# A two-layer mixer on one core: block-diagonal first stage for the filter, small vectors as rows, the MLP's first tokens in the written order

## The chip, the core and the metric

The kernel runs on one core of a Trainium2 chip. A core has five engines with an instruction stream each: PE (TensorE, matrix products into PSUM), DVE (VectorE), ACT (ScalarE), POOL (GpSimd) and SP (SyncE, which here issues nearly all DMAs). PE writes only to PSUM, and only DVE and ACT copy results out of it ("evacuate" it) into SBUF. The engines wait for one another through semaphores. The metric is the device time of one execution in microseconds; before the change the median of three runs is 253.25 us (252.85 to 253.61).

## The reference

Input and output are 2048 tokens of 512 values in bf16. Two kinds of layers alternate, A, B, A, B, each with a residual sum around it:

```python
def _A_ref(q, k, v, shift_k, ssm_k, ssm_D):
    k_shift = sum over t < 4 of k[s - t] * shift_k[:, t]     # four taps per channel
    kv = k_shift * v
    y = irfft(rfft(kv, 4096) * rfft(ssm_k, 4096))[:2048]     # long causal convolution, per channel
    return q * (y + kv * ssm_D)

def _B_ref(x, w1, b1, w2, b2):
    return gelu(layernorm(x) @ w1 + b1) @ w2 + b2            # 512 -> 1376 -> 512

x = A_q
x = x + _A_ref(_layernorm(x), A_k, A_v, ...)
x = x + _B_ref(_layernorm(x), B_w1, ...)
x = x + _A_ref(_layernorm(x), A_k, A_v, ...)
x = x + _B_ref(_layernorm(x), B_w1, ...)
```

(The listing is cut and its sums are put in short.) Everything in A but its q is the same for both A layers, so y is computed once.

## The kernel before

The work has two parts. The first computes y, in an order that is written out by hand; the second runs both MLPs over four groups of 512 tokens each, twice (eight rounds).

**First part.** The long convolution is a transform of 2048 = 32 x 64 points done with products. For kv and for the filter A_ssm_k alike, a first stage multiplies by a small table (32 points), a second by twiddled tables (64 points); the two spectra are multiplied, and two more stages go back. The 512 channels go in four chunks of 128, numbered cc = 0 to 3. The pieces have names, and a piece that ends in "e" is the evacuation of the piece without the "e":

- lk, lv, lK, lx, lM, lW, lX, w1, w2 and so on: loads, issued by SP. lSK loads a row of A_shift_k, lsT the same data as columns, lb0 and lb1 the MLP's bias as columns.
- kT: transposes of k (PE); dg: diagonal matrices from the taps; kv: the four taps as products with these diagonals; kvm: the product with v (DVE). Channels of chunk 3 take another way: POOL's multiplications kg, ka, kgm with the taps spread by bSK.
- U{cc}S: first stage of kv, U{cc}T its transposes (chunk 3 by DMA); KS{c}{g}: first stage of the filter, sixteen pieces; K2: its second stage; sa, sb: two DMA copies that swap halves.
- X{cc}{j}: second stage of kv; T{cc}{j}: the multiplication of the spectra (DVE); V{cc}{j}: the third stage; Z and TA to TD: turns, by DMA or PE; Y: the last stage.
- s00, s01, s02: statistics, scale and application of the first norm of tokens 0 to 511; s10, s11 the statistics and scale for tokens 512 to 1023. g, h, p, b: gating, statistics, scale and application of the second norm of tokens 0 to 511, in units of 1, 1 and 2 tiles of 128 tokens; LT their transposes for the MLP.

The string ORDER sets the order: a word such as `KS11.P3` or `U2T1e.A` names a piece, its engine (S, P, D, A, G for POOL) and, for PE, which of four PSUM buffers of 1024 columns it takes. Each engine runs its pieces in that order; the waits follow from what is read and written. All big arrays lie in one SBUF tile, `arena`, at byte offsets given by hand, and a place is used again by other data as the work goes on. The row of A_ssm_D, which the filter needs early, is parked in it ahead of everything else, with a DMA that ACT issues (L186), and POOL copies it into the tile Dz (L194):

```python
SKr = at(82 * K, [[1, P * KS]], 0, 1)
nc.scalar.dma_start(apf(arena, 40 * K, [[32 * ROW, 4], [1, D]]), apf(A_ssm_D, 0, [[0, 4], [1, D]]))
```

`at` counts bytes and `apf` counts elements of two bytes, so the second line's 40 K is byte offset 80 K; its four rows lie on partitions 0, 32, 64 and 96.

**Second part.** A round multiplies by W1 (L686; eleven tiles of 128 columns, four products each), applies gelu on ACT with the bias (L688), and multiplies by W2 (L720); DVE adds the result to x (L725). Two rounds ahead, `prep` does the norms of a group on DVE, with one small power on POOL, and turns it by DMA (L712). Round 0 is cut in three units that follow the end of the first part.

Of the kernel before, what the change touches and what calls it, by code (L numbers as in the profile page):

```python
# [29 lines left out]
def _make_tables():  # L30
# [43 lines left out]
    F = np.concatenate([F2, np.tile(KF, (4, 1))], axis=1)  # L74
# [30 lines left out]
def kernel(ctx: ExitStack, tc: tile.TileContext, A_q, A_k, A_v, A_shift_k, A_ssm_k, A_ssm_D,  # L105
                 B_x, B_w1, B_b1, B_w2, B_b2, out):
    nc = tc.nc
    P = 128
# [55 lines left out]
    SKr = at(82 * K, [[1, P * KS]], 0, 1)  # L164
    one = const.tile([1, P], BF16, name="one")
    kh = const.tile([P, KS - 1, P], BF16, name="kh")
    sT = const.tile([P, CT, KS], BF16, name="sT")
# [641 lines left out]
```

## Time and profile before

| | |
|---|---|
| median of the runs | 253.25 us |
| span of the profiled execution | 251.9 us |
| its own time | not on the page; taken to be that of the runs, so that some 1.3 us lie around the span |
| first part, until the first product of L720 | 106.4 us |
| seven and a half rounds after it | 145.5 us |
| PE, DVE, ACT, POOL busy, share of the span | 94%, 67%, 58%, 22% |
| granted PE clock | full throughout |

A row of the timeline gives the start, the time, the engine and line, the operation, what is written and read, and in brackets how long the engine had been idle and what ended that. A "q" after an engine (SPq, ACTq) marks the issue of a DMA. A share of busy time is an average over stages that have different limits, so the stages are looked at one by one.

### The profile page before, as it was taken

The numbers are of one execution on the slowest core, as the hardware profiler recorded it, in microseconds if no ns is written. First come the engines' busy times: TensorE is split into PE (matmuls) and PEld (weight loads), VectorE is DVE, ScalarE is ACT, GpSimd is POOL, SyncE is SP. The second block draws the span as 40 slices with busy tenths as digits, with TensorE's granted clock in tenths as the row PEclk, the third lists the DMA queues.
The fourth block names the chain that finished last, engine by engine and source line by source line (L and its number), as shares of the span: only waits on it lengthen the run. The fifth ranks groups of instructions, "written<-read, shape, count | busy, mean of one in ns | idle before, by whom it ended". The sixth has DMA issues, their size and how long they took to land.

```text
span 251.9 us, 5135 instructions
## 1 busy us (share of the span) xinstructions
PE 236.9 (94%) x2104; PEld 146.1 (58%) x2104; DVE 169.7 (67%) x319; ACT 146.5 (58%) x212; POOL 54.6 (22%) x52
## 2 busy tenths in 40 slices
PE   2688999999999999999999999999999999999995
PEld 1588767899998738844444444444444444444443
DVE  0335889989999794987889899886866862022022
ACT  3598899999999798903803803803703712712810
POOL 3199999510000011011111101110110110000000
DMA  5999994698929993022040403107006006001001
GB/s 130 367 349 183 239 428 191 209 390 300 232 44 181 175 318 113 0 48 39 1 83 0 86 0 61 22 0 86 1 28 139 3 25 143 0 23 64 0 21 62
DMA packets 53040, 30.15 MB, mean 120 GB/s; under 512 B 46642, under 2 KB 50456, under 8 KB 51736
## 3 DMA queue, kind: packets, MB, share of 16 engines
q1 hardware_dynamic: 52864, 29.73, 45.0%
q8 instruction: 16, 0.26, 0.4%
q10 hardware_dynamic: 152, 0.09, 0.1%
q14 instruction: 8, 0.07, 0.1%
HBM read 16.71 MB, written 2.10 MB: 75 GB/s over the span
## 4 chain that ended last, share of the span: by engine, by line
PE 70%; DVE 9%; ACT 8%; DMA 8%; issue 4%; ACTq 0%; SPq 0%; DVEq 0%
PE po L720 30%; PE ph L686 29%; DVE arena L218 4%; DMA arena<-in_A_q_dram 3%; DMA arena<-in_B_w_dram 3%; DVE T L555 2%; PE p L506 2%; PE p L336 2%; ACT arena L216 2%; ACT ZT L216 2%; DVE ZT L218 2%; DMA arena<-in_A_ssm_D_dram 2%; ACT xb L216 2%; ACT arena L469 1%; PE p L382 1%
## 5 line engine op out<-in xcount | busy, mean ns | idle before, releaser
L688 ACT ACTIVATE arena<-ph,B 128x512 bf16<-128x512 f32 (+5 forms) x110 | 63.5, 609 | 81.9 <-PE ph L686 81.8
L686 PE MATMUL ph<-arena 128*128 128x512 bf16 (+4 forms) x440 | 78.5, 336 | 0.9 <-DMA arena<-in_B_w_dram 0.5
L720 PE MATMUL po<-arena 128*128 128x512 bf16 (+2 forms) x363 | 77.4, 372 | 0.0
L686 PEld LDWEIGHTS <-arena 128*128 128x128 bf16 (+1 forms) x440 | 40.5, 100 | 38.0 <-DMA arena<-in_B_w_dram 1.0
L720 PEld LDWEIGHTS <-arena 128*128 128x128 bf16 (+1 forms) x363 | 35.4, 98 | 40.5
L725 DVE TENSOR_TENSOR arena<-po,arena 128x512 bf16<-128x512 f32 (+1 forms) x33 | 21.5, 673 | 43.6 <-PE po L720 43.6
L216 ACT ACTIVATE arena<-p 128x1024 bf16<-128x1024 f32 (+6 forms) x40 | 38.8, 1040 | 7.9 <-PE p L423 4.5
L250 POOL TENSOR_TENSOR lrsm<-lrsm,mhalf 128x4 f32<-128x4 f32 (+2 forms) x10 | 8.9, 885 | 96.6 <-DVE lrsm L244 96.6
L216 ACT ACTIVATE ZT<-p 128x1024 bf16<-128x1024 f32 (+1 forms) x22 | 21.6, 1038 | 0.1
L238 DVE BATCH_NORM_STATS2 lstm<-arena 128x6 f32<-128x512 bf16 x32 | 19.9, 681 | 0.2
L218 DVE CAST arena<-p 128x1024 bf16<-128x1024 f32 x15 | 17.8, 1221 | 1.6 <-PE p L382 1.4
L555 DVE TENSOR_TENSOR T<-xb,arena 128x2048 bf16<-128x2048 bf16 (+1 forms) x17 | 18.8, 1163 | 0.0
L564 PE MATMUL p<-arena,T 128*128 128x128 bf16 x256 | 16.5, 219 | 1.1 <-DVE arena L218 0.4
L250 POOL TENSOR_TENSOR lrsg<-lrsg,mhalf 128x4 f32<-128x4 f32 x8 | 8.1, 1014 | 40.8 <-DVE lrsg L247 40.8
L437 POOL TENSOR_TENSOR T<-arena,SK 128x2048 bf16<-128x2048 bf16 (+3 forms) x4 | 15.0, 3751 | 5.1 <-DMA arena<-in_A_k_dram 5.0
L216 ACT ACTIVATE xb<-p 128x1024 bf16<-128x1024 f32 x15 | 15.9, 1132 | 0.1
L564 PEld LDWEIGHTS <-T 128*128 128x128 bf16 x256 | 14.9, 98 | 1.7 <-issue 1.4
L238 DVE BATCH_NORM_STATS2 lstg<-arena 128x6 f32<-128x512 bf16 x24 | 14.8, 680 | 0.0
L218 DVE COPY arena<-p 128x2048 bf16<-128x2048 bf16 (+3 forms) x10 | 10.4, 1049 | 5.9 <-issue 3.7
L255 DVE TENSOR_SCALAR arena<-arena,lmvg,lrsg 128x512 bf16<-128x512 bf16 x28 | 9.7, 408 | 6.7 <-POOL lrsg L250 6.7
L255 DVE TENSOR_SCALAR arena<-arena,lmvm,lrsm 128x512 bf16<-128x512 bf16 x32 | 11.2, 409 | 2.3 <-POOL lrsm L250 2.3
L506 PE MATMUL p<-DG,arena 128*128 128x128 bf16 x192 | 11.4, 219 | 1.3 <-ACT ZT L216 0.9
(78 smaller groups left out, 222.8 us busy)
## 6 DMA issues: line engine op xcount, KB each, us to landing
arena<-arena SPq DMA_DIRECT2D x8, 512.0 KB, 4.5
arena<-in_A_k_dram SPq DMA_DIRECT2D x4, 512.0 KB, 6.7
arena<-in_A_v_dram SPq DMA_DIRECT2D x2, 1024.0 KB, 10.8
arena<-in_A_ssm_k_dram SPq DMA_DIRECT2D x4, 512.0 KB, 7.1
arena<-tabM SPq DMA_DIRECT2D x1, 2048.0 KB, 12.5
arena<-in_A_q_dram SPq DMA_DIRECT2D x1, 2048.0 KB, 9.1
out_dram<-arena SPq DMA_DIRECT2D x15, 128.0 KB, 1.7
arena<-in_B_w_dram SPq DMA_DIRECT2D x1, 1376.0 KB, 7.8
```

Source lines behind the costliest of these rows:

```text
L216: nc.scalar.activation(dst, src, AF.Copy)
L218: nc.vector.tensor_copy(dst, src)
L238: nc.vector.bn_stats(self.st[:, i, 0, :], x_t[:, GT * g + i, :] if src is None else src[:, i, :])
L250: nc.gpsimd.tensor_tensor(self.rs[:, a:b], self.rs[:, a:b], mhalf[:, a:b], ALU.pow)
L255: nc.vector.tensor_scalar(out=dst[:, i, :], in0=xs, scalar1=self.mv[:, i, 0:1], scalar2=self.rs[:, i:i + 1], op0=ALU.subtract, op1=ALU.mult)
L506: nc.tensor.matmul(o[:, i, :], w, DG[:, cc, t, :], start=t == 0, stop=t == KS - 1)
L555: eng.tensor_tensor(view(Tb[it["slot"]["T"]], [2, n, CW]), x2, kk, ALU.mult)
L564: nc.tensor.matmul(o[:, i, :], T[:, r, i, :], Mt[:, ka + i, 1 - r, :], start=r == 0, stop=r == 1)
L686: nc.tensor.matmul(o.rearrange("p (i t) -> p i t", t=P), W1t[:, ct, ft * P:ft * P + m], lt[:, a:b, ct, :], start=ct == 0, stop=ct == CT - 1)
L688: nc.scalar.activation(hT[0:m, ft, a * P:b * P], o, AF.Gelu_apprx_tanh, bias=B1[0:m, ft:ft + 1])
L720: nc.tensor.matmul(po[:, a:b], hT[0:m, ft, i * P:(i + 1) * P], W2t[0:m, ft, a:b], start=ft == 0, stop=ft == FT - 1)
L725: nc.vector.tensor_tensor(xs, po[:, a:b], xs, ALU.add)
```

## The change

- The table for the filter's first stage becomes block-diagonal: one product of all 128 rows with 256 columns takes the place of four pieces of 32 rows and 64 columns; the product with the identity that came ahead of each group (L377) goes. A step handles four blocks for all rows instead of eight for half of them.
- The taps are loaded as one row of 2048 values and turned to columns by twelve products with one column each (bS); the bias likewise by eleven (bB). The loads lsT, lb0, lb1 in columns and POOL's copies sF and B1 go.
- The MLP's first 512 tokens (transposes LT1, LT2, products M, gelu Me) come into the written order and use its PSUM buffers.
- x is loaded in two pieces (lx, ly); the statistics of tokens 512 to 1023 (LG1) are taken from ly at the end of the first part instead of from a load of their own; the separate load lx1 and s10, s11 go.
- The order is another.

SP's first loads before, in order (the word behind "waits" is the semaphore; DMAHW0 to DMAHW7 are eight DMA semaphores that are used in turn, DMAHW1 first by the load of A_ssm_D):

```order
L280 DMA arena<-in_A_shift_k_dram 1x512
L280 DMA arena<-in_A_k_dram 128x2048
L280 DMA sT<-in_A_shift_k_dram 128x4x4
L280 DMA arena<-in_A_k_dram 128x2048 x3
L280 DMA kh<-in_A_k_dram 112x3x128 [waits DMAHW0_49]
```

and in the changed kernel:

```order
L279 DMA arena<-in_A_shift_k_dram 1x2048 [waits DMAHW1_49,Pool_49]
L279 DMA arena<-in_A_k_dram 128x2048 x4
L279 DMA kh<-in_A_k_dram 15x3x128
L279 DMA kh<-in_A_k_dram 112x3x128 [waits DMAHW0_49]
L279 DMA arena<-in_B_b_dram 1x1376
```

The first load has got a wait for the load of A_ssm_D and for POOL, since its row now begins at 80 KB; the load of sT is gone, and the bias comes early.

ACT's work behind the statistics s00, before (ZT is the first stage of kv, 128x64x8x2 are the filter's pieces KS):

```order
L472 ACTIVATE arena,aq_124<-arena,as_123 128x512 x4
L216 ACTIVATE ZT_95<-p_119 128x4x8x32
L216 ACTIVATE ZT_95<-p_121 128x4x8x32
L490 ACTIVATE arena<-arena,am_125,lrsg_106 128x512 x4
L216 ACTIVATE ZT_96<-p_122 128x4x8x32
```

and after:

```order
L423 ACTIVATE DG<-IDt,sF 128x128 x12
L215 ACTIVATE arena<-p_117 128x4x3x128
L475 ACTIVATE arena,as_121<-arena 128x512 x4
L476 ACTIVATE as_121<-as_121 128x4
L478 ACTIVATE arena,aq_122<-arena,as_121 128x512 x4
L215 ACTIVATE ZT_93<-p_117 128x4x8x32
L215 ACTIVATE ZT_94<-p_119 128x4x8x32
L215 ACTIVATE ZT_94<-p_120 128x4x8x32
```

The application of the first norm (L490, s02) has left ACT; it stands on DVE behind the last multiplication T. The diagonals (DG) have come to ACT. In the same way U2T1e has gone from ACT to DVE.

ACT at the end of the first part, before (ph are the PSUM tiles of the MLP) and after (p the four buffers of the first part):

```order
L216 ACTIVATE arena<-p_122 128x1024
L216 ACTIVATE arena<-p_120 128x1024
L216 ACTIVATE arena<-p_121 128x1024
L688 ACTIVATE arena<-ph,B_77 128x128 x8
L216 ACTIVATE arena<-po 128x512
L688 ACTIVATE arena<-ph,B_77 128x128 x2
L688 ACTIVATE arena<-ph,B_77 96x128
```

```order
L215 ACTIVATE arena<-p_118 128x1024
L697 ACTIVATE arena<-p_119,B_76 128x128 x2
L697 ACTIVATE arena<-p_119,B_76 96x128
L697 ACTIVATE arena<-p_117,B_76 128x128 x8
L215 ACTIVATE arena<-p_118 128x1024
L215 ACTIVATE arena<-p_120 128x512
L697 ACTIVATE arena<-p_119,B_76 128x256 x4
```

The first gelu pieces now stand between the evacuations of Y instead of behind all of them, and the tokens come in the order 128 to 255, 256 to 511, 0 to 127.

The diff, cut to its core:

```diff
 ORDER = """
-lSK.S lk1.S lsT.S lk3.S lk0.S lk2.S bSK.P3 lh1.S bSKe.A lh113.S lx0.S kT1.P2 lv0.S sF.G lv1.S dg0.D dg2.D ...
+lSK.S bSK.P0 bSKe.A bS.P2 lk3.S lk1.S lk0.S lk2.S lh113.S bSe.A dg2.A dg0.A dg1.A lh1.S kg0.G kT3.P2 ...
 """
-    F = np.concatenate([F2, np.tile(KF, (4, 1))], axis=1)
+    F = np.concatenate([F2, np.kron(np.eye(4), KF)], axis=1)
...
-    SKr = at(82 * K, [[1, P * KS]], 0, 1)
+    SKr = at(80 * K, [[1, D * KS]], 0, 1)
+    b1r = at(85 * K, [[1, FT * P]], 0, 1)
...
-        lS = [load("lsT", sT[:], A_shift_k.rearrange("(ct p) k -> p ct k", p=P), 2 ** 17),
-              load("lSK", SKr, apf(A_shift_k, CK * P * KS, [[P * KS, 1], [1, P * KS]]), 2 ** 13)]
+        lS = [load("lSK", SKr, apf(A_shift_k, 0, [[D * KS, 1], [1, D * KS]]), 2 ** 13),
+              load("lb1", b1r[:, 0:F], apf(B_b1, 0, [[F, 1], [1, F]]), 2 ** 13)]
...
-        sf = plan.add("sF", {"G": 100}, lS[:1], lambda it: nc.gpsimd.tensor_copy(sF[:], sT[:]))
+
+        def columns(o):
+            for ct in range(CK):
+                for t in range(KS):
+                    nc.tensor.matmul(o[:, ct * KS + t:ct * KS + t + 1], at(80 * K + 2 * (ct * P * KS + t), [[KS, P]], 0, 1),
+                                     one[0:1, 0:1], start=True, stop=True)
+        _, sf = mm_evac("bS", 700, lS[:1], columns, [CK * KS], lambda: sF[:])
...
-                    nc.tensor.matmul(o[:, 0, :, :].rearrange("p m k -> p (m k)")[:, 0:320], IDt[:], Ft[:], start=True, stop=True)
-                    for m in range(8):
-                        for e in range(2):
-                            rs = slice(64 * g + 32 * e, 64 * g + 32 * e + 32)
-                            s0 = 16 * c + 2 * m
-                            nc.tensor.matmul(o[:, e, m, :], Kd[rs, s0:s0 + 2, :].rearrange("p s b -> p (s b)"), Ft[rs, 256:320],
-                                             start=True, stop=True)
...
+                    for m in range(4):
+                        s0 = 2 * (m0 + m)
+                        nc.tensor.matmul(o[:, m, :], Kd[:, s0:s0 + 2, :].rearrange("p s b -> p (s b)"), Ft[:, 256:512],
+                                         start=True, stop=True)
...
-        s10, _ = first(1, x1, lx1)
...
-        lx = load("lx", x_t[:], q_d.rearrange(TOK, p=P), 2 ** 21, USp)
+        lx = load("lx", x_t[:, 0:GT, :], xd[:, 0:GT, :], 2 ** 19, USp)
+        ly = load("ly", x_t[:, GT:, :], xd[:, GT:, :], 3 * 2 ** 19, USp)
...
+        def head(n, part, f0, f9, deps):
...
+            pe = plan.add(f"M{n}{part}", {"P": 218 * (b - a) * (f9 - f0)}, deps, mms, take=["ps"])
...
+                    nc.scalar.activation(hT[0:m, ft, a * P:b * P], o[0:m, ft - f0, :], AF.Gelu_apprx_tanh, bias=B1[0:m, ft:ft + 1])
+            plan.add(f"M{n}{part}e", {"A": 250 * (b - a) * (f9 - f0)}, [pe, sb] + wd, gelu, free=[(pe, "ps")])
...
+        plan.add("LG1", {"D": 2950}, [ly], lambda it: (LG[1].part(1, 0, GT), LG[1].join(0, GT)))
...
-                for (a, b), nxt in zip(UNITS, UNITS[1:] + (None,)):
-                    mm1(0, a, b, 0, FT - 3)
...
+                one_ = prep(1)
+                LG[1].scale(0, GT)
+                for f in one_[1:] + pr[:1]:
+                    f()
                 mm2(0, 0, False, pr[1:])
```

More of the change, by code (lines that the diff above doesn't have):

```diff
@@ L404 @@
                        for w, a in (("a", 0), ("b", 1))])
-        _, bSK = mm_evac("bSK", 250, lS[1:2], lambda o: nc.tensor.matmul(o, one[:], SKr, start=True, stop=True), [P * KS],
+        _, bSK = mm_evac("bSK", 250, lS[:1], lambda o: nc.tensor.matmul(o, one[:], SKr[:, CK * P * KS:], start=True, stop=True), [P * KS],
                          lambda: SK[:])
@@ L455, in stats @@
             return plan.add(name, {"D": 670 * (b - a) + 150 + 40 * (b - a)}, deps, fn)
-        x1 = view(Tb[1], [GT, D])
         xd = q_d.rearrange(TOK, p=P)
         lx0 = load("lx0", lna0, xd[:, 0:GT, :], 2 ** 19)
-        lx1 = load("lx1", x1, xd[:, GT:2 * GT, :], 2 ** 19)
         def first(n, x, ld):
@@ L491, in first @@
             return s0, plan.add("s02", {"D": 1350, "A": 2200}, [s1], apply) if n == 0 else s1
-        _, s2 = first(0, lna0, lx0)
-        s10, _ = first(1, x1, lx1)
+        s0, s2 = first(0, lna0, lx0)
+        for it in sum(KX, []):
+            it["deps"] += [s0, bSK, sf, sb]
         kvp, USp, ZU = [], [], []
@@ L641 @@
         UNITS = (0, 1), (1, 2), (2, 4)
+        norm = []
         for n, (a, b) in enumerate(UNITS):
@@ L661 @@
             gb = plan.add(f"b0{a}", {"D": 350 * m}, [gp], lambda it, a=a, b=b: LM[0].apply(lnx[0], 0, a, b))
+            norm.append(gb)
             if n == 0:
-                mm_evac("LT0", 240, [gb], lambda o: turn_x(o, 0, 1), [1, CT, P], lambda: lnT[0][:, 0:1, :, :], True,
-                        edeps=wd, rank=1)
+                lt0 = mm_evac("LT0", 240, [gb], lambda o: turn_x(o, 0, 1), [1, CT, P], lambda: lnT[0][:, 0:1, :, :], True,
+                              edeps=wd, rank=1)[1]
         for g in range(1, 4):
```

69 lines of the change are left out of this document (41 added, 28 removed).

## The prediction

> **What bounds the kernel now.** I read the view by windows first, then the chain that ended last, then the timeline of the first 20 us, and last ScalarE (ACT) by itself. The windows are cut where the stages meet; after the two times stand the busy us of PE, PE's weight loads, VectorE (DVE), ACT and POOL, then the granted PE clock, the DMA share and GB/s.
>
> ```profile
> core 0 of [0], span 251.9 us
> 0.00:13.22 13.22, 5.63 (x49) 4.39 (x50) 2.42 (x13) 6.21 (x6) 4.21 (x18) 1.00 0.81 257
> 13.22:19.95 6.73, 6.40 (x104) 6.15 (x105) 3.09 (x4) 6.26 (x18) 6.73 (x3) 1.00 1.04 302
> 19.95:30.00 10.05, 9.18 (x176) 7.99 (x176) 7.06 (x6) 8.09 (x11) 9.64 (x9) 1.00 1.14 190
> 30.00:82.37 52.37, 50.20 (x879) 43.98 (x872) 49.26 (x51) 51.82 (x57) 18.61 (x9) 1.00 0.82 252
> 82.37:106.40 24.03, 22.86 (x244) 17.48 (x242) 18.51 (x37) 20.96 (x45) 2.32 (x4) 1.00 0.62 153
> 106.40:251.90 145.50, 142.59 (x671) 66.06 (x669) 89.33 (x213) 53.17 (x79) 13.09 (x13) 1.00 0.19 41
> ```
>
> From 106.4 us to the end PE does nothing but the MLP:
>
> ```profile
> 86.98 7.79 DMA arena<-in_B_w_dram
> ...
> 106.37 9.51 PE po L720 x44
> 115.89 9.50 PE ph L686 x44
> ```
>
> Phases of 9.5 us follow each other without a gap. The change adds or removes no product there, so I cost this part at nothing: the kernel gains or loses exactly by how much the first product of L720 moves from 106.37 us. Ahead of it, between 30 and 82.37 us, ACT is busy 51.82 of 52.37 us, more than PE (50.20, with modelled ends) and DVE (49.26). ACT's list of PSUM evacuations is therefore my measure of that stretch, not PE.
>
> The span is 251.94 us and the median of the runs 253.25, so 1.3 us lie outside the first and last instruction; I leave them as they are and take differences from the median.
>
> **The change part by part: the head.** The rows are those of the first 17 us.
>
> ```profile
> 0.80 0.35 SPq L280 DMA_DIRECT2D arena<-in_A_shift_k_dram  x1
> 1.18 1.21 ACTq L186 DMA_DIRECT2D arena<-in_A_ssm_D_dram  x1
> 1.21 0.38 SPq L280 DMA_DIRECT2D arena<-in_A_k_dram  x1
> 2.11 0.58 PE L407 MATMUL p<-arena,one 1*128 1x512 bf16 x1 [2.11 <-DMA arena<-in_A_shift_k_dram]
> 5.25 0.19 POOL L192 MEMSET arena<- 128x96 bf16 x1 [3.20 <-DMA arena<-in_A_ssm_D_dram]
> 5.37 1.41 POOL L194 COPY Dz<-arena 1x128 bf16<-1x128 bf16 x4
> 8.85 15.70 SPq L353 DMA_DIRECT2D arena<-in_A_ssm_k_dram  x4
> 11.89 0.85 PE L423 MATMUL p<-IDt,arena 128*128 128x128 bf16 x12 [0.28 <-DMA arena<-in_A_k_dram]
> 16.01 1.23 DVE L512 TENSOR_TENSOR arena<-p,arena 128x1024 bf16<-128x1024 f32 x1 [2.21 <-DMA arena<-in_A_v_dram]
> ```
>
> The new row of A_shift_k is 4 KB at 80 KB of partition 0, exactly where the row of A_ssm_D is parked (the old 1 KB row lay at 82 KB). So SP's first load now waits until A_ssm_D has landed and POOL has made its first copy of it; behind it in SP's queue stand all loads of k, q, v and the filter. When does it go? A_ssm_D is issued at 1.18; it lands at 2.5 at the earliest (a small load took 2.11 - 0.80 = 1.31 us) and at 5.2 as now. Now it shares the engines with SP's loads; then it is alone behind one table, which took 1.9 us to land (below). I take 1.18 + 1.9 = 3.1, plus 0.19 and one copy of 1.41 / 4 = 0.35: 3.65 us. The first load of k follows 0.41 later at 4.06 instead of 1.21: 2.85 us late (2.3 to 5.0).
>
> Against that, the small pieces go: the load of sT (512 pieces of 8 bytes) stood between the first two loads of k.
>
> ```profile
> 2.00:4.00 2.00, 0.58 (x1) 0.00 (x0) 0.00 (x0) 1.57 (x3) 0.05 (x1) 1.00 0.92 228
> 4.00:6.00 2.00, 0.47 (x5) 0.47 (x6) 0.00 (x0) 0.40 (x1) 0.71 (x3) 1.00 0.68 139
> 8.00:10.00 2.00, 1.12 (x11) 1.13 (x12) 1.11 (x7) 0.48 (x1) 0.00 (x0) 1.00 1.03 407
> ...
> Ft<-tabF ACTq DMA_DIRECT2D x1, 80.0 KB, 1.9
> sT<-in_A_shift_k_dram SPq DMA_DIRECT2D x1, 4.0 KB, 4.5
> ```
>
> While sT was on its way the engines moved 139 GB/s, later 407. The 2.1 MB of k are now complete 11.89 - 1.21 = 10.7 us after the first issue. Without sT I take 0.55 us to the first byte, 2 us at 300 GB/s, the other 1.5 MB at 407 (3.7 us) and 1.7 us to the signal: 8.0 us, so 12.05 instead of 11.89, and with what follows (a transpose batch of 0.85, eleven one-column products for the MLP's bias ahead of the convolution on PE) I take +0.4 us. The ends: nothing recovered +2.85, or +5.0 with the late landing; all at 407 GB/s, -0.5. *By a rule of the Trainium skill (DMA: Bandwidth & Descriptors, Specifications) transfers under 512 bytes are done as read-modify-write; by it the slow stretch belongs to sT, and the term would be about +0.2; the 139 GB/s row agrees, but does not part it from a slow start of the loads themselves.*
>
> The diagonals move from DVE to ACT and wait for twelve one-column products instead of sT. Prices: a one-column product between 0.02 us (16 pieces in 0.34, below) and 0.1, so bS and bB at most 1.2 us each; a diagonal on ACT between the 2.0 / 12 that it cost on DVE and 2.18 / 8.
>
> ```profile
> L417 DVE TENSOR_SCALAR DG<-IDt,sF 128x128 bf16<-128x128 bf16 x12 | 2.0, 248 | 7.1 <-POOL sF L361 7.1
> 95.31 2.18 ACT L688 ACTIVATE arena<-ph,B 128x128 bf16<-128x128 f32 x8 [0.82 <-PE ph L686]
> ```
>
> A_shift_k arrives at 3.65 + 1.31 = 4.96, bSK and bS end by 6.7, twelve diagonals at 0.27 by 10.0: before the last k, which hides them. The second load of v now stands behind two filter loads of 15.70 / 4 = 3.9 us of SP each, so it is issued near 16.5 and lands about 22; the new order asks for it only at 23 (all first halves of the convolution come first). If that cover fails it costs 1 to 2 us of DVE.
>
> **Filter's first stage.** PE's pieces of the chain:
>
> ```profile
> 24.73 0.87 PE p L304 x8
> ...
> 35.53 0.24 PE p L377
> 35.77 0.34 PE p L382 x16
> ```
>
> A step was 0.34 + 0.24 = 0.58 us; it becomes four products of the shape of L304, 0.87 / 2 = 0.44. Sixteen steps give PE back 2.2 us, less about 0.7 for the bias. The evacuation stays 1024 columns per step, on ACT or DVE, so PE waits for it: on the path this is worth nothing by itself. *The Trainium skill (TensorE: Matmul & The Clock Gate, Part 3) says the opposite of this change: four products of 32 rows each run side by side, 3.07 times as fast. Worked out as an estimate, the full-array form would cost 0.34 x 3.07 = 1.04 us per step, 7.4 us more over sixteen, and the kernel would be slower. The rows of L304 decide against it: that shape takes 0.44, the old pieces being only 64 columns wide.*
>
> **ACT from 19.95 to 82.37 us.** Busy 8.09 + 51.82 = 59.9, idle 2.5.
>
> ```profile
> 22.58 2.93 ACT L490 ACTIVATE arena<-arena,am,lrsg 128x512 bf16<-128x512 bf16 x4 [0.72 <-POOL am L482]
> 52.07 1.88 ACT L216 ACTIVATE arena<-p 128x2048 bf16<-128x2048 bf16 x1
> 78.80 3.57 ACT L216 ACTIVATE ZT<-p 128x1024 bf16<-128x1024 f32 x4
> ```
>
> The normalisation of the first 512 tokens leaves (2.93, to DVE after the multiplications), so does the evacuation U2T1e (1.88, to DVE); evacuations of 1024 columns go from 58 to 59 (+0.9, 3.57 / 4). That is -3.9. DVE takes on 1.2 for U2T1e, loses one evacuation (1.1) and the statistics of the second 512 tokens (3.0), and fits: it was idle 3.1 of the 52.37 us, and more before. ACT's own waits at the start grow, since the evacuations it gets first come one by one behind the convolution: walking PSUM buffer by buffer I find some 3.4 idle for 2.5. Net -3.0 (from -4.9, were ACT never idle, to -1.5).
>
> **From there to 106.37.** It took 24.0 us. PE's and ACT's work is the same, only interleaved. Walking ACT's new list (last evacuation of V, then Y, transposes, 33 activations) with these prices and the latencies of the normalisation between, the last activation ends 24.3 us later; the first product of L720 needs its PSUM buffer. I take +0.25; the ends are -1.2 (PE's idle 24.03 - 22.86 all gone) and +1.5.
>
> ```profile
> 82.72 2.69 SPq L611 DMA_TRANSPOSE arena<-ZT  x2
> 85.50 2.41 SPq L280 DMA_DIRECT2D arena<-in_B_w_dram  x3
> ...
> 101.26 1.37 DVE L255 TENSOR_SCALAR arena<-arena,lmvg,lrsg 128x512 bf16<-128x512 bf16 x4
> 110.63 2.47 DVE L238 BATCH_NORM_STATS2 lstg<-arena 128x6 f32<-128x512 bf16 x4
> 110.74 1.85 SPq L712 DMA_TRANSPOSE arena<-arena  x1
> 114.70 1.38 DVE L255 TENSOR_SCALAR arena<-arena,lmvg,lrsg 128x512 bf16<-128x512 bf16 x4 [1.12 <-POOL lrsg L250]
> ```
>
> W1 is issued behind five turns instead of eight, and behind a last multiplication that ends 3 us earlier: near 79, to land by 87 (7.79 as now); its first use is near 88. The statistics LG1 now stand on DVE after the last normalisation of the first tokens: 114.70 - 110.63 = 4.1 us to the next step, then 110.74 - 101.26 = 9.5 to the turn and 4.3 for it, 18 in all. PE has 9 us of products left in front of L720 there and 9.5 of L720 itself, so they just fit; what exceeds it delays the second L686 phase.
>
> The other edits lie beside work that covers them, and I cost them at nothing: the load of x in two pieces is needed only after 82 us, the 1376 two-byte pieces of the bias go from a stretch in which ACT and not DMA is full, and POOL loses two copies of 0.2 that nothing waited long for.
>
> The sum: +0.4 - 3.0 + 0.25 = -2.35, so 250.9 us.
>
> **Rivals.** *Slower, by the head:* if the slow start is the loads' own, all of the 2.85 us stays; then -2.35 + 2.45 gives 253.35, and with A_ssm_D as late as today (2.15 more) 255.5. From a head loss of 3.5 us on, the kernel is slower. For it: 228 GB/s also before sT's turn. Against: 139 falls in sT's time alone. *The end does not follow:* W1 comes only three turns of 1.35 earlier than now, at 94.8 - 4.0 = 90.8; PE then waits 2 us and the time is 252.9. For it: the transfers ran at full share there. Against: the issue had waited for the turns only. *More gain:* the head all recovered (-0.5), ACT without more idle (-3.9), the end -0.3: 248.6 to 249.4. For it: PE's needs shrink by 2.2 too. Against: both evacuating engines must stay full. *The rule of the small products:* 257 by PE, against the rows.
>
> **How the numbers follow.** Forecast 0.47, more gain 0.22, W1 late 0.15, head 0.15, the rule 0.01. The forecast alone spans 250.0 to 251.9. The range goes from 249.0 (a third of the more-gain case lies below) to 253.9 (two thirds of the head case above). Within 0.3% (0.76 us) a measurement of this kernel tells nothing: 252.5 to 254.0 is "same". Faster: 0.46 + 0.22 + 0.03 of W1 = 0.71; same: 0.10 of W1, 0.03 of the head, 0.01 = 0.14; slower 0.15.
>
> **What would show it.** In the changed profile: SP's first load at 3 to 4 us behind POOL's copy; the last k batch on PE near 12; ACT's last V evacuation near 79.8; W1 in no wait above 0.5 us; the first product of what is now L720 near 104. I am wrong if the k loads land after 13.5, if ACT is idle more than 5 us between 20 and 80, or if PE waits for W1 or for the second 512 tokens.

## The result: slower, and the profile after

The changed kernel takes 256.75 us (255.78 to 257.82, four executions) where the kernel before takes 253.31 beside it: a ratio of 1.0143, with a 95% interval of 1.0107 to 1.0179. I had said 250.9, faster. Executions of the kernel before come with a mean granted PE clock of either 0.998 to 1.000 or 0.985 to 0.993, and the latter are some 2.8 us longer; "at the full clock" below means a mean of at least 0.996, and the changed kernel was at 0.991 to 0.993 in all four executions.

The profiled execution has a span of 255.7 us (its own time 257.37). This is the view by windows, cut where the same four stages meet as in the prediction (after the two times: PE, its weight loads, DVE, ACT, POOL, granted clock, DMA share, GB/s):

```profile
core 0 of [0], span 255.7 us
0.00:21.70 21.70, 13.13 (x150) 11.99 (x151) 4.93 (x6) 13.49 (x34) 10.67 (x18) 1.00 0.83 227
21.70:30.00 8.30, 8.25 (x121) 7.67 (x119) 5.82 (x6) 4.59 (x7) 7.89 (x9) 1.00 1.07 234
30.00:83.09 53.09, 51.19 (x748) 46.09 (x745) 49.17 (x46) 51.84 (x58) 19.20 (x7) 1.00 0.81 244
83.09:109.58 26.49, 23.16 (x233) 18.68 (x238) 20.32 (x47) 20.78 (x47) 3.74 (x5) 0.94 0.58 149
109.58:255.70 146.12, 142.20 (x663) 66.07 (x669) 88.61 (x211) 54.95 (x80) 13.09 (x13) 1.00 0.18 40
```

The cuts before were 19.95, 82.37, 106.37 and 251.94, so each stage can be set beside its term:

| stage | before | after | difference | predicted |
|---|---|---|---|---|
| head, until ACT is through with s00 | 19.95 | 21.70 | +1.75 | +0.4 |
| ACT's stretch, until its last V evacuation | 62.42 | 61.39 | -1.03 | -3.0 |
| end, until the first product with W2 | 24.00 | 26.49 | +2.49 | +0.25 |
| MLP behind it | 145.57 | 146.12 | +0.55 | 0 |
| sum | 251.94 | 255.70 | +3.76 | -2.35 |

Two places carry it. The head first, in the timeline of PE and SP:

```profile
3.63 0.35 SPq L279 DMA_DIRECT2D arena<-in_A_shift_k_dram  x1
4.05 1.79 SPq L279 DMA_DIRECT2D arena<-in_A_k_dram  x4
13.73 1.46 PE L431 MATMUL p<-IDt,arena 128*128 128x128 bf16 x12 [0.22 <-DMA arena<-in_A_k_dram]
15.50 5.40 PE L513 MATMUL p<-DG,arena 128*128 128x128 bf16 x64
```

SP's first load goes at 3.63, as predicted (3.65). The last batch of k's transposes starts at 13.73, not 12.05. And PE is slow: these 12 transposes took 0.85 us before, and the first 64 products of the convolution took 3.75, as this row of the kernel before shows:

```profile
13.22 3.75 PE L506 MATMUL p<-DG,arena 128*128 128x128 bf16 x64 [0.47 <-ACT arena L216]
```

The second place is the end, in the timeline between the last turns and the MLP:

```profile
90.47 0.40 PE L642 MATMUL p<-IDt,arena 128*128 128x128 bf16 x4 [0.49 <-DVE arena L254]
91.54 0.10 PEld L689 LDWEIGHTS <-arena 128*128 128x128 bf16 x1 [0.30 <-DMA arena<-in_B_w_dram]
91.94 0.68 DVE L660 TENSOR_TENSOR arena<-arena,p 128x512 bf16<-128x512 bf16 x1
92.65 3.77 ACT L215 ACTIVATE arena<-p 128x512 bf16<-128x512 f32 x4 [2.13 <-DVE arena L660]
93.79 4.24 PE L689 MATMUL p<-arena 128*128 128x128 bf16 x44 [2.27 <-ACT arena L215]
```

W1 is there at 91.54. But ACT's next piece is Y00e, which copies the first tile of Y out of PSUM, and it waits 2.13 us for DVE's gating product g00 (L660), which reads the same PSUM buffer and stands in the order ahead of it. Behind Y00e on ACT stands LT1e, and PE's first MLP products M1a need that. PE stands still for 2.27 us, and then this happens to its clock (the third column from the end, by windows):

```profile
90.00:92.00 2.00, 1.04 (x7) 0.63 (x9) 1.97 (x8) 0.52 (x1) 0.00 (x0) 1.00 1.21 270
92.00:94.00 2.00, 0.21 (x4) 0.21 (x4) 1.97 (x6) 1.35 (x3) 0.70 (x1) 1.00 1.20 237
94.00:96.00 2.00, 2.00 (x24) 2.00 (x21) 0.66 (x3) 2.00 (x2) 1.07 (x2) 0.52 0.88 195
96.00:98.00 2.00, 2.00 (x26) 2.00 (x24) 0.00 (x0) 0.42 (x1) 0.00 (x0) 0.62 1.04 354
98.00:100.00 2.00, 1.95 (x19) 1.21 (x18) 1.42 (x3) 1.93 (x8) 0.00 (x0) 1.00 0.39 132
```

At half clock the time under it is (0.48 x 2 + 0.38 x 2) / 0.5 = 3.4 us. The Trainium skill (TensorE: Matmul & The Clock Gate, Part 1) describes a gate that halves the clock after an idle window of about 3.4 us and gives it back after a busy one. The 3.4 us of low clock agree with that window; the pause that set it off was no whole idle window (PE worked 1.04 us between 90 and 92 and 0.21 between 92 and 94).

The 0.55 us that the MLP takes longer lie behind its last addition on DVE: from there to the end of the span it is 3.04 us (252.66 to 255.70), before 2.45. It is 2.9 to 3.0 us in every trace with the new order and 2.4 to 2.5 in every trace with the old one; what takes it I have not looked into.

### The profile page after: what moved, and what is told of

It reads as the page before. It is cut to its first block, busy times and chain, and to the rows that moved or that the text cites. A ratio compares the mean times of both kernels' runs of the same rounds, so it can differ in the third digit from the quotient of the medians.

```text
span 255.7 us, 4760 instructions
## 1 busy us (share of the span) xinstructions
PE 237.9 (93%) x1907; PEld 150.5 (59%) x1919; DVE 168.9 (66%) x312; ACT 145.6 (57%) x221; POOL 54.6 (21%) x50
## 4 chain that ended last, share of the span: by engine, by line
PE 78%; DMA 8%; ACT 5%; DVE 5%; issue 1%; SPq 1%; POOL 0%; ACTq 0%
PE po L760 30%; PE ph L726 26%; PE p L689 5%; PE p L513 4%; DMA arena<-ZT 4%; ACT arena L215 4%; DMA arena<-in_A_k_dram 3%; PE p L335 2%; PE p L543 2%; PE p L403 2%; ACT ZT L215 2%; PE p L303 1%; PE p L567 1%; PE p L634 1%; PE p L602 1%
## 5 line engine op out<-in xcount | busy, mean ns | idle before, releaser
L728 ACT ACTIVATE arena<-ph,B 128x512 bf16<-128x512 f32 (+1 forms) x77 | 52.7, 687 | 78.9 <-PE ph L726 78.9
L760 PE MATMUL po<-arena 128*128 128x512 bf16 (+3 forms) x355 | 77.0, 372 | 0.4
L726 PE MATMUL ph<-arena 128*128 128x512 bf16 (+1 forms) x308 | 67.6, 379 | 0.0
L760 PEld LDWEIGHTS <-arena 128*128 128x128 bf16 (+1 forms) x363 | 35.4, 98 | 40.7
L726 PEld LDWEIGHTS <-arena 128*128 128x128 bf16 (+1 forms) x308 | 30.8, 100 | 35.9
L215 ACT ACTIVATE arena<-p 128x1024 bf16<-128x1024 f32 (+7 forms) x41 | 38.2, 1020 | 8.1 <-DVE arena L660 2.1
L217 DVE COPY arena<-p 128x2048 bf16<-128x2048 bf16 (+4 forms) x13 | 12.9, 996 | 20.0 <-PE p L431 13.3
L237 DVE BATCH_NORM_STATS2 lstg<-arena 128x6 f32<-128x512 bf16 x28 | 17.2, 679 | 0.0
L217 DVE CAST arena<-p 128x1024 bf16<-128x1024 f32 x13 | 15.3, 1219 | 0.7 <-PE p L390 0.6
L689 PE MATMUL p<-arena 128*128 128x128 bf16 (+3 forms) x132 | 11.8, 260 | 2.3 <-ACT arena L215 2.3
L513 PE MATMUL p<-DG,arena 128*128 128x128 bf16 x192 | 13.2, 235 | 0.0
## 6 DMA issues: line engine op xcount, KB each, us to landing
arena<-in_A_ssm_k_dram SPq DMA_DIRECT2D x4, 512.0 KB, 10.2
```

What stands on the lines that cost most here:

```text
L215: nc.scalar.activation(dst, src, AF.Copy)
L217: nc.vector.tensor_copy(dst, src)
L237: nc.vector.bn_stats(self.st[:, i, 0, :], x_t[:, GT * g + i, :] if src is None else src[:, i, :])
L513: nc.tensor.matmul(o[:, i, :], w, DG[:, cc, t, :], start=t == 0, stop=t == KS - 1)
L689: nc.tensor.matmul(o[0:m, ft - f0, :].rearrange("p (i t) -> p i t", t=P), W1t[:, ct, ft * P:ft * P + m], lnT[0][:, a:b, ct, :], start=ct = ...
L726: nc.tensor.matmul(o.rearrange("p (i t) -> p i t", t=P), W1t[:, ct, ft * P:ft * P + m], lt[:, a:b, ct, :], start=ct == 0, stop=ct == CT - 1)
```

## Experiments

### Head and end, one by one and together

The first kernel parks the row of A_ssm_D where nothing lies yet (the start of the arena), in both lines that name the place:

```
-    nc.scalar.dma_start(apf(arena, 40 * K, [[32 * ROW, 4], [1, D]]), ...
+    nc.scalar.dma_start(apf(arena, 0, [[32 * ROW, 4], [1, D]]), ...
-        nc.gpsimd.tensor_copy(..., apf(arena, 40 * K + 32 * cg * ROW + cg, ...
+        nc.gpsimd.tensor_copy(..., apf(arena, 32 * cg * ROW + cg, ...
```

> The changed kernel, with the row of A_ssm_D parked at the start of the arena (free until the filter's second stage) instead of at 80 KB, so that the row of A_shift_k no longer lies over it and SP's first load waits for nothing. Theory 'head': the wait for that landing and for POOL's copy is what the head lost. SP's first load then goes at 0.8 us instead of 3.63, the last batch of k's transposes starts on PE near 11 instead of 13.73, and the time falls by 1.8 to 2.5 us, to 254.3 to 255.0. Rival 'not the head': the loads of k are limited by their own start or by PE's state, the last batch moves by less than 0.7 us, and the time stays within 0.8 us of 256.75.

Measured: 253.43 us (251.17 to 255.3, ten executions), 3.3 less. At the changed kernel's clock (0.991 to 0.993) the median is 253.9, that is 2.9 less; four executions kept the full clock, with a median of 251.8. Most of the wide spread is the clock. In its timeline:

```profile
0.80 0.35 SPq L279 DMA_DIRECT2D arena<-in_A_shift_k_dram  x1
1.21 1.90 SPq L279 DMA_DIRECT2D arena<-in_A_k_dram  x4
10.97 1.46 PE L431 MATMUL p<-IDt,arena 128*128 128x128 bf16 x12 [0.15 <-DMA arena<-in_A_k_dram]
```

The last batch comes 2.76 us earlier than in the changed kernel, with the first load 2.83 earlier. The head theory holds, with more gain than I expected; it is 9.7 us from the first issue of k to the last transposes in both kernels. Part of the gain may be PE's: in this execution the first 64 products of the convolution took 3.75 us, in the changed kernel's 5.40.

The second kernel moves one word, so that ACT's evacuation no longer waits for DVE:

```
- ... Y10e.A h02.D g00.D TC2.P3 Y00e.A w1.S LT1.P0 ...
+ ... Y10e.A h02.D TC2.P3 Y00e.A g00.D w1.S LT1.P0 ...
```

> The changed kernel, with DVE's gating product g00 written behind ACT's evacuation Y00e instead of ahead of it. In the changed kernel ACT's Y00e waited 2.13 us for g00 (both read the same PSUM buffer), LT1e stood behind it, PE stood still from 91.5 to 93.79, and then the granted clock was 0.5 until 97.5. Theory 'one evacuation': Y00e runs near 90.6, LT1e by 91.5, the MLP's first products start between 91.5 and 92 (W1 landed at 91.54), the pause of PE is under 1 us and the clock stays at 1.0; the time falls by 2.0 (start alone) to 3.8 us (with the clock). Rival 'W1 next': W1 lands at 91.5 or later because the transfers are full there, PE's pause stays above 1.5 us, the clock still drops, and the gain is under 1.5 us. Rival 'nothing': the later units of the same tokens take over, the gain is under 0.5 us.

Measured: 252.77 us (252.03 to 254.1), 4.0 less, and all ten executions at the full clock.

PE's timeline and, below it, the window that showed 0.52:

```profile
91.43 2.62 PE L689 MATMUL p<-arena 128*128 128x128 bf16 x44
```
```profile
94.00:96.00 2.00, 1.95 (x18) 1.22 (x17) 1.92 (x6) 1.96 (x9) 1.07 (x2) 1.00 0.42 104
```

M1a starts 2.36 us earlier and takes 2.62 instead of 4.24 us: 2.36 + 1.62 = 3.98, the whole gain. W1, my own rival, takes none of it: the products follow PE's other work without a pause.

> Both edits (row of A_ssm_D parked elsewhere; g00 behind Y00e). If the head and the end are separate losses, their gains add: 256.75 minus the sum of what the two single kernels gained, near 251.5 (250.5 to 253). If they are one loss (the end only waits for transfers that the head delayed), the gain is that of the larger alone, 253 to 254.5.

Measured: 250.1 us (249.83 to 251.1), 6.65 less, where the two single gains add to 7.3. Against the kernel before the ratio is 0.9868 (0.9818 to 0.9918), and against its executions at the full clock (median 252.77) it is 2.7 us. They are two separate losses, and without them the change does gain.

### Is it the pause or the slow clock behind it?

Here 36 products whose result nobody reads are put where PE stands still at the end, in a PSUM buffer that the next evacuated piece uses anyway:

```
+plan.add("wmE", {"P": 2000}, [], lambda it: [
+    nc.tensor.matmul(view(pf[it["slot"]["ps"]], [P]), IDt[:], IDt[:], start=True, stop=True) for _ in range(36)], take=["ps"])
- ... LT1e.A Y12.P1 ...
+ ... LT1e.A wmE.P1 Y12.P1 ...
```

> The changed kernel with 36 additional 128x128 products on PE (results never read) put where it stands still near 91 us, before the MLP's first products. Nothing starts earlier: the wait for Y00e and g00 stays. Theory 'the pause lowers the clock': the granted clock stays 1.0 from 94 to 98, the first 44 MLP products take 2.6 us instead of 4.24, and the time falls by 1.4 to 2.2 us, to 254.5 to 255.4, with the wait itself still paid. Rival 'the clock falls for another reason' (or costs nothing): the clock still shows 0.5 there, or the time stays within 0.7 us of 256.75.

Measured: 254.26 us (253.94 to 254.83), 2.5 less, by additional work, and all ten executions at the full clock. PE's timeline, and the same window:

```profile
89.70 2.17 PE L418 MATMUL p<-IDt 128*128 128x128 bf16 x36
92.78 2.62 PE L691 MATMUL p<-arena 128*128 128x128 bf16 x44
```
```profile
94.00:96.00 2.00, 2.00 (x34) 1.88 (x33) 0.05 (x1) 1.98 (x5) 0.88 (x2) 1.00 0.94 283
```

The first theory holds: the pause lowers the clock. Y00e still waits for g00 (2.17 us here). M1a's 44 products save 1.62 us. The rest of the 2.5 is not accounted for by the clock: in this execution M1a began 1.0 us earlier than in the changed kernel. Here the first 64 products of the convolution took 3.75 us without any filling, and not 5.40; the next experiment looks at that.

### Does the slow start of PE in the head cost anything?

The same kind of filling, in the pauses of the head (20, 8 and 10 products around the batches of transposes):

```
- bSK.P0 bSKe.A bS.P2 ... kT3.P2 kT1.P0 ... kT2.P2 ...
+ bSK.P0 bSKe.A bS.P2 ... wm0.P3 kT3.P2 wm1.P3 kT1.P0 ... wm2.P3 kT2.P2 ...
```

> The changed kernel, with 38 additional 128x128 products on PE in the pauses while it waits for k (20, 8 and 10 of them, results never read); nothing else changes, the loads come as late as before. Theory 'cold PE': the first 64 products of the convolution took 5.40 us instead of 3.75, and the last 12 transposes of k 1.46 instead of 0.85, because PE had stood still too much before them. With PE kept at work these come back: 3.75 and 0.85, and the time falls by 1 to 2.3 us, to 254.5 to 255.8. Rival 'late k only': the products are slow for another reason (their operands arrive late, or ports are shared with the transfers); the 64 products still take over 5 us and the time stays within 0.7 us of 256.75.

PE's timeline:

```profile
13.56 0.84 PE L434 MATMUL p<-IDt,arena 128*128 128x128 bf16 x12 [0.26 <-DMA arena<-in_A_k_dram]
14.69 3.75 PE L516 MATMUL p<-DG,arena 128*128 128x128 bf16 x64
93.38 3.97 PE L692 MATMUL p<-arena 128*128 128x128 bf16 x44 [2.27 <-ACT arena L215]
```

PE does what the theory says, 0.84 and 3.75 us, and the convolution's first 64 products end 2.5 us earlier. The time does not follow: 256.44 us (254.44 to 257.83). At 93 us only 0.4 is left of that. DVE's timeline shows where it goes; the changed kernel comes first, then this one:

```profile
26.98 1.23 DVE L519 TENSOR_TENSOR arena<-p,arena 128x1024 bf16<-128x1024 f32 x1 [0.62 <-PE p L513]
```
```profile
27.34 2.35 DVE L522 TENSOR_TENSOR arena<-p,arena 128x1024 bf16<-128x1024 f32 x2 [2.66 <-DMA arena<-in_A_v_dram]
```

This is the first multiplication that needs the second load of v. With the slow PE it waited for PE; with the faster one it waits 2.66 us for that load, which SP issues behind the filter's first loads (at 18.90, in the changed kernel at 18.64), and starts no earlier. Put on top of the two edits that gained:

> All three edits together: the row of A_ssm_D parked elsewhere, g00 behind Y00e, and the 38 additional products that keep PE at work while k arrives. With the first two alone (250.1 us) the profile still shows the first 64 convolution products in 5.54 us. Theory 'cold PE costs': they take 3.75 again and 0.6 us of the last transposes comes back; one run with early loads and a PE that had warmed up by itself had its later stages 1.1 us earlier; so 248.9 to 249.5. Rival 'hidden': POOL, the filter's loads and ACT set the pace behind the head anyway; within 0.4 us of 250.1.

Measured: 250.53 us (250.27 to 250.7). Once more both, on one chip:

> The changed kernel with the two edits that gained (row of A_ssm_D parked elsewhere, g00 behind Y00e), a second time, beside the next kernel on the same chip: 249.8 to 251.

> The same with the 38 additional products at the head. If a PE that is slow for its first products costs anything at the end, it is 0.6 to 1.2 us faster than the run beside it; if POOL, the loads of the filter and ACT set the pace behind the head, within 0.4 us of it.

Measured: 250.11 us (249.59 to 250.17) without and 250.72 (249.81 to 250.85) with the filling, 0.6 more, which neither theory had. In the profile of the former PE had come to full speed by itself (3.75 us), so this pair does not set a slow PE against a fast one; and its second load of v goes at 16.29 and the multiplication starts at 23.87, with the filling 17.55 and 25.43. So the filling gains nothing. That a slow PE costs nothing is not shown: of the kernel with two edits one trace has the 64 products in 5.54 us (251.1 us in all), the other in 3.75 (250.13). What hides the faster PE I only read from the traces: the second load of v. No experiment here issues it earlier.

### What the parts of the change are worth

With both losses out, s02 goes back to ACT, near 22 us as before the change, on top of the kernel with all three edits (250.53 us beside it):

```
- ... s02.D TC0be.A ...
- ... kvm11.D s01.G U1S1e.A ...
+ ... kvm11.D s01.G s02.A U1S1e.A ...
```

> e5_all with s02, the normalisation of the first 512 tokens (2.93 us on ACT in the kernel before), back on ACT behind s01, near 22 us, instead of on DVE near 80. My prediction counted its leaving as 2.93 us gained, because ACT was taken to be the bound of that stretch. Theory 'ACT was the bound': the time rises by 2 to 3 us, to 251 to 252.2. Rival 'it filled a pause': ACT waits for PE there anyway (three pauses of 0.8 to 1.8 us between 19 and 33 us), so the time rises by less than 1 us, to at most 250.2.

Measured: 250.99 us (250.58 to 252.06), 0.5 more. ACT's timeline:

```profile
22.57 2.92 ACT L499 ACTIVATE arena<-arena,am,lrsg 128x512 bf16<-128x512 bf16 x4
25.39 1.01 ACT L215 ACTIVATE ZT<-p 128x1024 bf16<-128x1024 f32 x1
26.29 0.46 ACT L215 ACTIVATE arena<-p 128x64 bf16<-128x64 f32 x1
```

ACT has 2.92 us of work more and the next evacuation but one, of 128x64, ends 2.03 us later (24.26 + 0.46 beside it); at 39 us ACT is 1.05 later (38.80 for 37.75), of which 0.4 stood there before s02. By the medians of four the price is 0.5, so for the most part it filled a pause, as the rival said; the two profiled executions themselves lie further apart (252.06, the slowest of its four, and 250.27).

Then the filter's first stage in its old form (16 products of 32 rows a step, from the block-diagonal table's blocks), everything else the same:

```
-for m in range(4):
-    nc.tensor.matmul(o[:, m, :], Kd[:, s0:s0 + 2, :]..., Ft[:, 256:512], ...)
+nc.tensor.matmul(o[:, 0, :, :]...[:, 0:320], IDt[:], Ft[:, 0:320], ...)
+for m in range(8):
+    for e in range(2):        # rs: 32 rows; q = 2 * g + e
+        nc.tensor.matmul(o[:, e, m, :], Kd[rs, s0:s0 + 2, :]..., Ft[rs, 256 + 64 * q:320 + 64 * q], ...)
```

> e5_all with Filter's first stage in its old form, one opening product and 16 products of 32 rows per step instead of four block-diagonal ones (a step 0.58 us of PE instead of 0.44, 16 steps). My prediction said: 2.2 us of PE, worth nothing on the path because the evacuations set the pace. By that: within 0.5 us of e5_all. Rival 'PE is the bound there' (PE is busy 0.97 of the time between 20 and 54 us): the time rises by 1.2 to 2.4 us.

Measured: 252.67 us (251.63 to 253.47), 2.1 more. The kernel with block-diagonal products comes first, the one with the small pieces second; shown is what PE does at the end of the first stage:

```profile
34.30 2.43 PE L390 MATMUL p<-Ft,arena 128*128 128x256 bf16 x20 [0.26 <-ACT arena L215]
36.80 1.03 PE L303 MATMUL p<-Ft,arena 128*128 128x256 bf16 x8
```
```profile
37.01 0.41 PE L393 MATMUL p<-Ft,arena 32*128 32x64 bf16 x16
37.35 0.31 PE L387 MATMUL p<-Ft,IDt 128*128 128x320 bf16 x1
38.32 1.05 PE L303 MATMUL p<-Ft,arena 128*128 128x256 bf16 x8
```

The eight products of kv's first stage that follow start 1.5 us later, of which 0.3 stood there before the filter's first stage began (23.05 for 22.71). Five block-diagonal steps in a row take 2.43 us, 0.49 each; a small step keeps its 0.58 (37.01 to 37.59). So PE's work counts on the path here, and PE, not ACT, was the bound; where the rest of the 2.1 us arises the traces do not show.

The same part alone, put into the kernel before:

> The kernel before with one part of the change alone: Filter's first stage as four block-diagonal products per step (and the table of 512 columns that they need), everything else and the order as before. My prediction said that on the path this is worth nothing; the same part taken out of the improved new kernel cost 2.1 us. Theory 'PE is the bound there in either order': it gains 1.2 to 2.2 us against the kernel before at the same granted clock. Rival 'only the new order turns it into time' (in the old order the steps lie one by one between ACT's and DVE's evacuations): within 0.6 us of the kernel before. Row tiles side by side 3.07 times as fast, as a page's rule has it, would make it several us slower.

Measured: 252.58 us (251.65 to 252.74), all ten executions at the full clock; the kernel before had 253.07 at the full clock and 255.4 to 256.9 in three of its 13. At the full clock it gains 0.5, so the rival is right for the old order: there a step waits for its evacuations. Its timeline shows such waits, 0.8 us in these two rows, where the view of the kernel before lists none between 27 and 40 us and the five steps above have 0.26:

```profile
35.12 1.92 PE L380 MATMUL p<-Ft,arena 128*128 128x256 bf16 x16 [0.52 <-ACT arena L216]
37.28 1.95 PE L380 MATMUL p<-Ft,arena 128*128 128x256 bf16 x16 [0.24 <-ACT arena L216]
```

### The head's wait in the old kernel, and the old kernel's clock

The one number that makes SP wait, put into the kernel before:

```
-SKr = at(82 * K, [[1, P * KS]], 0, 1)
+SKr = at(80 * K, [[1, P * KS]], 0, 1)
```

> The kernel before with its row of A_shift_k at 80 KB instead of 82 KB, so that it lies over the parked row of A_ssm_D as in the changed kernel and SP's first load waits for it; nothing else. Theory 'the wait alone costs what parking elsewhere gave back': SP's first load goes at 3.6 us, the last transposes of k start 2.5 to 3.3 us later than at 11.89, and the time rises by 2.5 to 3.5 us at the same granted clock. Rival: in the old order POOL's chain or the filter's loads hide a part; below 1.5 us.

Measured: 256.97 us (256.52 to 259.44); at the full clock 256.86 for 253.07, 3.8 more. SP's first load goes at 3.61. So in the old order the wait alone costs more than the whole slowdown of 3.4 us; in the new one it was 2.9 to 3.3. Its profiled execution had a mean clock of 0.987, and by windows it shows where the old order loses its clock:

```profile
36.00:38.00 2.00, 1.92 (x48) 1.33 (x44) 1.49 (x2) 2.00 (x3) 2.00 (x1) 1.00 1.04 434
38.00:40.00 2.00, 1.90 (x61) 1.18 (x59) 1.67 (x2) 1.77 (x4) 1.92 (x2) 1.00 1.07 451
40.00:42.00 2.00, 2.00 (x51) 1.33 (x45) 1.61 (x2) 1.66 (x3) 2.00 (x2) 0.61 1.01 434
42.00:44.00 2.00, 2.00 (x35) 1.11 (x34) 1.39 (x2) 1.18 (x2) 1.92 (x3) 0.50 0.89 365
44.00:46.00 2.00, 2.00 (x24) 1.43 (x24) 0.35 (x2) 1.78 (x2) 2.00 (x1) 0.50 0.20 74
46.00:48.00 2.00, 2.00 (x21) 1.27 (x21) 1.52 (x2) 1.05 (x2) 1.92 (x2) 0.68 0.00 0
```

and in PE's timeline what it did there, the last piece at full and the first at half clock:

```profile
39.85 0.40 PE L382 MATMUL p<-Ft,arena 32*128 32x64 bf16 x16
40.43 0.61 PE L382 MATMUL p<-Ft,arena 32*128 32x64 bf16 x16
```

PE is not idle: it is busy 1.90 to 2.00 of every 2 us. But from 37.66 on it does nothing but the filter's small pieces (16 products of 32 rows and 64 columns, then one of 128x320, over and over), and after some 3 us of them the clock is halved, for (0.39 + 0.5 + 0.5 + 0.32) x 2 / 0.5 = 6.8 us, twice the 3.4 seen above. With the part on block-diagonal products alone no execution of ten lost the clock; the kernel before lost it in 24 of the 57 beside all these experiments, in 3 of the 13 beside that one. Where those 24 lost it no trace shows, and the profiled execution of the kernel before has the same row of small pieces at the full clock. So the small pieces are the likely cause, not a shown one, and they do not bring it about every time; that they do not count as work for the clock is my reading.

## Why the prediction was wrong

**Head, +0.4 predicted, +1.75 measured.** The step that failed is "Without sT I take ... 8.0 us": the time from the first issue of k to the last transposes. That k starts at 4.06 was right (4.05). But from there it took 9.7 us (13.73 - 4.05), as it does in the first experiment (10.97 - 1.21); the kernel before needed 10.7. Taking sT away gave back 1.0 us and not 2.7. (The stage's end, s00, starts when q has landed, 15.17 for 13.43; q stands behind k in SP's queue.) The view by windows shows that the loads start slowly without sT too:

```profile
4.00:6.00 2.00, 0.73 (x11) 0.46 (x11) 0.00 (x0) 0.12 (x1) 0.64 (x2) 1.00 0.42 117
6.00:8.00 2.00, 0.21 (x7) 0.12 (x4) 0.00 (x0) 1.97 (x7) 0.00 (x0) 1.00 0.91 238
8.00:10.00 2.00, 1.46 (x12) 1.20 (x12) 0.24 (x1) 2.00 (x8) 0.00 (x0) 1.00 0.93 291
```

In steps of 1 us from the first issue of k the engines moved 8, 229, 225, 258, 254 and then 336 GB/s; in the kernel before it was 75, 250, 210, 92, 161 and then 262. I had put 300 from 0.55 us on and 407 two us later; the 0.55 us to the first byte and the 1.7 us to the signal were estimates that no row shown gives. I had read 139 GB/s beside sT as sT's doing, and named the other reading as the rival "the slow start is the loads' own", with 15%. It was right in the main: sT makes the dip deeper, but five slow microseconds stay without it. (The 228 GB/s that I set against the 139 fell in sT's time as well, 1.64 to 6.1 us.) The Trainium skill (DMA: Bandwidth & Descriptors, Specifications) has transfers under 512 bytes done as read-modify-write, and by it the slow stretch would have been sT's; the rates without sT decide against that use of the rule, not against the rule. The head's price by experiment is 2.9 to 3.3 us, and the rival's time for this loss alone, 253.35, is near what the kernel without the other loss takes (252.77).

**ACT's stretch, -3.0 predicted, -1.03 measured.** Two errors. ACT's busy time fell by 3.5 (59.9 to 4.59 + 51.84 = 56.4), near my 3.9. But its idle time rose from 2.5 to 5.0 where I had 3.4: between 21.7 and 30 ACT was busy 4.59 of 8.30 us and PE 8.25. The step "ACT's list of PSUM evacuations is therefore my measure of that stretch, not PE" fails at its start, where PE is the bound; its slow first products (5.40 us for 3.75) were in no term. With the head's wait gone the size does come out, but in one of two traces. These are rows of that one, the kernel with two edits (250.11 us), in its timeline:

```profile
19.27 0.19 ACT L478 ACTIVATION_READ_ACCUMULATOR arena<-arena,as 128x1 f32 x1
79.23 1.09 ACT L215 ACTIVATE arena<-p 128x768 bf16<-128x768 bf16 x2
87.68 2.63 PE L689 MATMUL p<-arena 128*128 128x128 bf16 x44
102.21 9.68 PE L760 MATMUL po<-arena 128*128 128x512 bf16 x44
```

From 19.46 to 79.23 it is 59.8 us, where the same view of the kernel before has 62.4 (20.04 to 82.41): 2.6 less. In the other trace, with the 64 products in 5.54 us, it is 61.6 (19.22 to 80.83), 0.8 less. And where the -3.0 is nearly met, it is by luck: s02 is worth 0.5 in the new order and not 2.9, and the part that I had put at "worth nothing by itself" is worth 2.1. Its price on PE was nearly right (0.58 to 0.44 a step; measured 0.49), and so was leaving the 3.07 of the row tiles aside.

**End, +0.25 predicted, +2.49 measured.** The step is the walk through ACT's list: it took Y00e to run when PE had its product, and did not count that g00, placed ahead of it in the order, reads the same PSUM buffer on DVE and makes ACT wait 2.13 us with LT1e behind. The slow clock that a pause brings (1.62 us) was in no term. Without both, the end is 102.21 - 79.23 = 23.0 us and shorter by 0.8 than in the same view before (106.21 - 82.41 = 23.8); here my walk erred to the other side.

**W1.** Predicted near 79 with landing by 87; it was issued at 84.43 and there at 91.54, since the three turns ahead of it kept SP from 79.00 to 83.85. That is 4.5 us later than predicted, and later than the rival's 90.8. It cost at most 0.3 us, because the transposes that M1a needs were later still.

**Right:** the place and the size of SP's new wait; the diagonals on ACT hidden (they end at 10.2, ahead of k); the second load of v, issued at 18.64 instead of 16.5 and in the changed kernel still waited for by nobody (in five of the seven traces with the head's loss out DVE does wait for it, 1.4 to 2.8 us, where I had named 1 to 2 for that case); LG1 and what follows it "just fit" (the next products with W1 start 9.5 us after the first with W2, without a gap); the MLP's products (from the first phase with W2 to the last it is 133.1 us in both kernels; the 0.55 us lie behind them).

The changed kernel without its two waits comes near the forecast of 250.9 (250.1), in part by the luck said above. The forecast was wrong in the two places where the change made an engine wait for another through a shared address: one that I saw and priced too low, one that I did not see; and it took ACT for the bound where PE was.

## What to carry to other kernels

When an order is rewritten, list for every PSUM buffer who reads it and on which engines; a cheap reader behind a late one on another engine stops its whole queue. Price a pause of PE at what follows it as well: here 2.3 us of waiting cost 4.0. A first load that is held costs its whole delay and more (2.8 us late, 2.9 to 3.8 lost), and whether an engine bounds a stretch is read in windows of 10 us, not 50. The best version here is the change with its two waits taken out: 250.11 us, a ratio of 0.984 (0.9771 to 0.991) to the kernel before, and 3.0 us less than its executions at the full clock (253.07). Its DVE still waits for the second load of v (1.43 us in its trace), so an earlier place for that load is the next thing to try.

## What the runs showed that I had not expected

- PE's clock falls without PE being idle: some 3 us of products of 32 rows and 64 columns, back to back and 95% busy, and then 6.8 us at half clock, in one trace. The executions of the kernel before with a lower mean clock were 2.7 to 2.9 us longer (medians 252.77 and 255.46 in the first group of 25 executions, 252.74 and 255.68 in the second of 19). In the new order the same small pieces kept the full clock in ten of ten executions; what sets the two apart stays open.
- The pause at the end does not cost the clock every time either: with the head's wait out and that pause still there (2.27 us in the trace), four of ten executions kept the full clock, and one of ten with the filling in the head.
- Useless products at the right place make the kernel faster by 2.5 us (at the end), and at another place, where they speed PE up just as well, they gain 0.3 us in the median (in the head) or nothing.
- The granted clock in the rows says 1.00 in the head, while the same 64 products take 3.75 or 5.40 us there. A slow PE at the start is seen in the mean times only.
